# Attention in units of 64 queries of four heads, with queries and keys in plain float32, in place of units of 128 queries of two heads in split float32r

## The chip, the cores and the metric

The kernel runs on one core of a Trainium2 chip. The metric is the time of one execution on the device, in microseconds. Three runs of the kernel before took 944.76, 943.54 and 944.8 us, median 944.76. TensorE is called PE here, VectorE DVE, ScalarE ACT, GpSimd POOL, and SP is the engine that issues the transfers.

## The reference

```python
# attention: q, k, v of (4 batches, 8 heads, 576 positions, 64 features)
scores = 0.125 * q @ k.T                    # per batch and head
scores = where((rel >= 0) & (rel < 128), scores - slope[h] * abs(rel), -1e9)   # rel = query - key
x = softmax(scores) @ v                     # 2304 tokens x 512 features
# first MoE layer, dense
h = x @ w_in                                # 512 -> 2048
x = maximum(0.01 * h, h) @ w_out            # 2048 -> 512
# second MoE layer: 8 experts, each token goes to one, 288 tokens an expert (greedy by logit)
logits = x @ w_gate
out[tokens of e] = maximum(x @ w1[e], 0) @ w2[e]
```

A query sees itself and the 127 positions before it, in its own batch of 576 positions. w_in and w_out are handed to the kernel as 64-bit floating-point numbers and become float32 on the chip, in pieces ("conversions", `conv_abs` to `in_low`). Routing is exact enough only with products near float32, so the MoE products are made of float32r parts: a value is a high part (a rounded copy, made by ACT) and a low part (the difference, made by DVE or POOL), and three products, high by high, low by high, high by low, stand for one.

## The kernel before

The 2304 tokens are 18 blocks of 128 queries (`NB`), counted through the four batches, so that a batch's end falls within blocks 4 and 13, at row 64. A *unit* is one block with one pair of heads: 72 units, four to a block. A step s of the loop at L664 takes unit s through the softmax and, at the same time, makes the scores of unit s + 1, the transposes of unit s - 1 and the products with v of unit s - 2. Beside them a step holds at most one *item*, 24 matmuls of the first MoE product (`expand`, L532), and at set step numbers the stages of a conversion (`conv_at`, steps 0 to 45, two steps in three), the gate's products made from w_out (`gate_transpose`, `gate_product`, `gate_fold`), and the logits (L559) and their folds (L570). An item of chunk c (two blocks) can start when the chunk's last products with v are done (`ready`). When the units end, items alone go on until L223, the second product, takes over at 444 us.

PE's and ACT's instructions run in the order in which the program writes them (`manual_schedule`); those of DVE, POOL and SP are put in order by a planner that estimates when each can run, and that lets a load wait for a free buffer while others pass.

The parts that the change touches:

- `load_half` (L315) loads queries and keys of half a block's heads, 64 features high, twice, into partitions 0 to 63 and 64 to 127. `split_half` (L403 to L417) copies the keys to the high part on ACT (L413) and subtracts for the low part (L414), both on all 128 partitions. Of the queries ACT makes the high part (L415) and L416 turns partitions 64 to 127 into the low part. The subtractions run on DVE for the first three halves (`SPLIT_V`) and on POOL after that.
- `scores` (L429): a head's query tile (high part over low part, 128 rows) meets the high keys and then the low keys, two float32r matmuls of 256 columns that add up, so four for a unit (L443). Where a block crosses a batch's end (`CUT`) a third matmul of one row adds a bias from `marks`. Blocks with fewer than 128 older keys of their batch take L448, a pair of matmuls for each part.
- `softmax_exp` and `softmax_norm`: for each head L464 scales, adds the bias and takes the minimum on DVE, L467 is the exponential on ACT with its sum, L475 and L476 make the reciprocal on DVE, and L478 multiplies.
- `transpose_p` (L488) makes four transposes of 128x128 for a unit; ACT copies them out (L491).
- `weighted` (L507): for each head and each of its two sets of 128 keys a plain float32 matmul of 128 queries into the partitions 0 to 63 or 64 to 127 of `xv`. A plain float32 matmul leaves two matmul records in the trace. In block 14, and 5, one set has 64 keys and stands between sets of 128.
- `bias_sb`: eight biases of 384 columns, two made on DVE and six on POOL (L632).
- POOL has, beside the splits, the sum of each conversion (L367) and the low part of w_in (L372).

Of the kernel before, what the change touches and what calls it, by code (L numbers as in the profile page):

```python
# [35 lines left out]
SPLIT_V = range(3)  # L36
# [40 lines left out]

OLD = [min(i * P % S, P) for i in range(NB)]  # L80
CUT = [S - i * P % S if S - i * P % S < P else None for i in range(NB)]


def _consts():
# [16 lines left out]
    rel = r[:, None] + P - np.arange(2 * P)[None, :]  # L101
    rel = np.where((rel >= 0) & (rel < WINDOW), -8.0 * rel, -2e12)
    add("rel", np.concatenate([rel, rel[:, :P]], axis=1))
# [15 lines left out]

_r, _cut = np.arange(P), next(c for c in CUT if c)  # L120
assert all(c in (None, _cut) for c in CUT)
MARKS = np.concatenate([_r >= _cut, np.full(P, -2e30), np.where(_r < _cut, -2e30, 0), np.full(P, -2e30)])
MARKS = MARKS[None].astype(mybir.dt.np(BF16))


@with_exitstack
def tile_attn_moe_moe2(ctx: ExitStack, tc: tile.TileContext, qk, v, w_in, w_out, w_gate, w1, w2, consts, mark_rows, out):
# [175 lines left out]
    with ExitStack() as actx:  # L303
        apool = actx.enter_context(tc.tile_pool(name="apool", bufs=2))
        marks = apool.tile([1, 4 * P], BF16, name="marks", bufs=1)
# [7 lines left out]
        half, vtile, qtile, raws = {}, {}, {}, {}  # L313

        def load_half(i, hf):  # L315
            if i < NB:
                t = apool.tile([P, 2, 4, P], F32, tag="qk", name=f"qk_{i}_{hf}", bufs=3)
                src = qk[i, :, :, 4 * hf:4 * hf + 4, :]
                nc.sync.dma_start(t[:D], src)
                nc.sync.dma_start(t[D:], src)  # L320
                half[i, hf] = t

        def load_v(i):
            if i < NB:
                for j, n in ((0, P),) + (((1, P - CUT[i]),) if CUT[i] else ()):
                    t = apool.tile([P, DM], F32, tag="v", name=f"v_{i}_{j}", bufs=4)
                    nc.sync.dma_start(t[:n], v[(i + 1) * P - n:(i + 1) * P, :])
                    vtile[i, n] = t
# [74 lines left out]
        def split_half(i, hf):  # L403

            if i >= NB:
                return
            if hf == 0:
                qtile[i] = apool.tile([P, H, P], F32R, tag="qs", name=f"qs_{i}")
            t, qs = half.pop((i, hf)), qtile[i]
            hs = slice(4 * hf, 4 * hf + 4)  # L410
            kh, kl = (r[:, hs, i % 2, :] for r in kring)
            eng = V if 2 * i + hf in SPLIT_V else GP
            A.activation(kh, t[:, 1], AF.Copy)  # L413
            eng.tensor_tensor(out=kl, in0=t[:, 1], in1=kh.bitcast(F32), op=ALU.subtract)  # L414
            A.activation(qs[:, hs, :], t[:, 0], AF.Copy)  # L415
            eng.tensor_tensor(out=qs[D:, hs, :], in0=t[D:, 0], in1=qs[D:, hs, :].bitcast(F32),  # L416
                              op=ALU.subtract)  # L417

        def keys_of(i):

            keys = [(i % 2, 0, vtile[i, P], P)]
            if OLD[i]:
                old = ((i - 1) % 2, P - OLD[i], vtile[i - 1, OLD[i]], OLD[i])
                keys = keys + [old] if OLD[i] == P and i % 2 == 0 else [old] + keys
            return keys

        st = {}

        def scores(u):  # L429
            i, c = u  # L430
            keys = keys_of(i)
            s = bank("s", "s_%d_%d" % u).rearrange("p (h k) -> p h k", h=2)
            whole = OLD[i] == P
            for h in range(2):
                hd = 2 * c + h
                q = qtile[i][:, hd, :]
                if whole:
                    ends = [(q, r[:, hd].rearrange("p a k -> p (a k)")) for r in kring]
                    if CUT[i]:
                        bo = P * (i % 2 == 0)  # L440
                        ends.append((marks[:, :P], marks[:, P + bo:3 * P + bo]))
                    for x, (a, b) in enumerate(ends):
                        T.matmul(s[:, h, :], a, b, start=(x == 0), stop=(x == len(ends) - 1))  # L443
                    continue
                ko = 0
                for slot, kc, _, kn in keys:
                    for x, ring in enumerate(kring):
                        T.matmul(s[:, h, ko:ko + kn], q, ring[:, hd, slot, kc:kc + kn],  # L448
                                 start=(x == 0), stop=(x == 1))
                    ko += kn  # L450
            st[u] = dict(keys=keys, whole=whole, s=s)

        def softmax_exp(u):
            i, c = u
            d = st[u]
            nk = P + OLD[i]
            bo = P if d["whole"] and i % 2 == 0 else P - OLD[i]
            nm_ = "%d_%d" % u
            neg = apool.tile([P, 2, 256], F32, tag="neg", name=f"neg_{nm_}")
            nm = apool.tile([P, 2], F32, tag="nm", name=f"nm_{nm_}", bufs=4)  # L460
            sm = apool.tile([P, 2], F32, tag="sm", name=f"sm_{nm_}", bufs=4)
            pr = apool.tile([P, 2, 256], F32, tag="pr", name=f"pr_{nm_}", bufs=PRB)
            for h in range(2):
                V.tensor_tensor_reduce(  # L464
                    out=neg[:, h, :nk], in0=d["s"][:, h, :nk], in1=bias_sb[:, 2 * c + h, bo:bo + nk],
                    scale=-0.125, scalar=3e38, op0=ALU.add, op1=ALU.min, accum_out=nm[:, h:h + 1])
                A.activation(pr[:, h, :nk], neg[:, h, :nk], AF.Exp, scale=-1.0, bias=nm[:, h:h + 1],  # L467
                             accum_out=sm[:, h:h + 1])
            d.update(nk=nk, sm=sm, pr=pr)

        def softmax_norm(u):
# [5 lines left out]
            for h in range(2):  # L477
                V.tensor_scalar(pr[:, h, :nk], pr[:, h, :nk], rs[:, h:h + 1], None, op0=ALU.mult)  # L478

        def transpose_p(u):  # L480
            d = st[u]
            keys, pr = d["keys"], d["pr"]
            pt = bank("t", "pt_%d_%d" % u).rearrange("p (h b q) -> p h b q", h=2, b=2)
            pts = apool.tile([P, 2, 2, P], F32, tag="pts", name="pts_%d_%d" % u, bufs=PTB)
            ko = 0
            for kb, (_, _, _, kn) in enumerate(keys):
                for h in range(2):
                    T.transpose(pt[:kn, h, kb, :], pr[:, h, ko:ko + kn], ident)  # L488
                ko += kn
            if d["whole"]:  # L490
                A.activation(pts, pt, AF.Copy)  # L491
            else:
                for kb, (_, _, _, kn) in enumerate(keys):
                    A.activation(pts[:kn, :, kb, :], pt[:kn, :, kb, :], AF.Copy)
# [4 lines left out]
        def weighted(u):  # L499
# [3 lines left out]
            if c == 0:  # L503
                xv[i] = bank("v", f"xv_{i}", bufs=1).rearrange("p (c q) -> p c q", c=4)
# [639 lines left out]
```

## Time and profile before

| | |
|---|---|
| profiled execution | 944.32 us, of which the span of instructions 942.5 |
| median of three runs | 944.76 us (943.54 to 944.8) |
| PE busy | 885.2 us, 94% |
| DVE busy | 634.0 us, 67% |
| ACT busy | 414.8 us, 44% |
| POOL busy | 211.9 us, 22% |
| mean granted clock of PE | 0.986 |

A busy time is the time in which an instruction of that engine is in progress. Matmuls overlap and their ends are modelled, so a PE that is busy all the time need not be at its peak: the distance from one start to the next tells how fast it goes. A DVE instruction that is held up counts as busy while it is held; the same instruction's shorter cases show what it needs. In a row of a group "xcount | busy, mean ns of one | idle before" follow the names and shapes.

### The profile page before, as it was taken

How to read it: one execution, taken by the hardware profiler on the slowest of the kernel's cores; microseconds unless marked ns; L12 is line 12 of the kernel's file. 1: busy time of each engine (PE TensorE's matmuls, PEld its weight loads, DVE VectorE, ACT ScalarE, POOL GpSimd, SP SyncE). 2: the span in 40 equal slices, each digit the busy share in tenths (PEclk: the TensorE clock that was granted, in tenths of full speed). 3: DMA queues.
4: the chain of work that ended last, by engine and by line, in shares of the span. 5: the costliest groups of instructions: out<-in, count | busy, mean ns of one | idle time of the engine just before them, and what ended most of it. 6: DMA issues, size and time to landing. Idle time of an engine off the chain costs nothing.

```text
span 942.5 us, 17809 instructions
## 1 busy us (share of the span) xinstructions
PE 885.2 (94%) x6886; PEld 759.8 (81%) x6886; DVE 634.0 (67%) x1569; ACT 414.8 (44%) x865; POOL 211.9 (22%) x198
## 2 busy tenths in 40 slices
PE   2677999999999999999999999998999999999996
PEld 2455888999898888898777766775789999999995
DVE  6999999999965455435877877777316455555550
ACT  5555665667654445434212121211215555565551
POOL 4565554454422222000000000000011211122211
PEclk9998899999999999999999999999999999999998
DMA  9555486787549965246332434221325556666540
GB/s 253 157 139 151 114 224 191 215 237 213 176 118 262 244 170 141 81 134 192 122 136 78 136 100 135 90 80 67 101 92 176 190 169 191 223 207 192 181 134 26
DMA packets 100727, 146.98 MB, mean 156 GB/s; under 512 B 6561, under 2 KB 64162, under 8 KB 100642
## 3 DMA queue, kind: packets, MB, share of 16 engines
q1 hardware_dynamic: 97570, 136.40, 49.6%
q0 software_dynamic: 3072, 9.44, 2.9%
q8 instruction: 54, 0.88, 0.4%
q14 instruction: 31, 0.25, 0.1%
HBM read 113.04 MB, written 32.77 MB: 155 GB/s over the span
## 4 chain that ended last, share of the span: by engine, by line
PE 80%; DVE 14%; issue 4%; POOL 1%; DMA 1%; ACT 0%; SPq 0%; POOLq 0%; DVEq 0%; ACTq 0%
PE po L223 21%; PE h L532 19%; PE m L1024 10%; PE y L1043 10%; PE xv L507 4%; PE s L443 3%; PE cnt L844 3%; PE pt L488 3%; PE lg L559 2%; DVE dt L357 2%; DVE pr L478 2%; DVE rs L475 2%; DVE neg L464 1%; DVE dt L355 1%; DVE de L365 1%
## 5 line engine op out<-in xcount | busy, mean ns | idle before, releaser
L223 PE MATMUL po<-wh_out,gol 128*128 128x512 f32 x272 | 112.6, 414 | 4.6 <-DVE gol L191 4.6
L223 PE MATMUL po<-wh_out,goh 128*128 128x512 f32 x272 | 111.0, 408 | 0.0
L223 PE MATMUL po<-wl_out,goh 128*128 128x512 f32 x272 | 110.6, 407 | 0.0
L532 PE MATMUL h<-xh,wh_in 128*128 128x256 f32 x576 | 100.1, 296 | 0.0
L532 PE MATMUL h<-xl,wh_in 128*128 128x256 f32 x576 | 92.9, 284 | 3.2 <-DVE xl L518 3.2
L532 PE MATMUL h<-xh,wl_in 128*128 128x256 f32 x576 | 92.6, 283 | 0.0
L183 ACT ACTIVATE goh<-gin 128x1024 fp32r<-128x1024 f32 x34 | 36.0, 1060 | 124.8 <-DMA gin<-g_dram 112.0
L160 DVE TENSOR_TENSOR wl_w<-st_w,wh_w 128x1024 fp32r<-128x1024 f32 x60 | 72.9, 1224 | 25.9 <-ACT wh_w L159 25.9
L545 DVE TENSOR_TENSOR gb<-h,th 128x512 f32<-128x512 f32 x72 | 49.4, 686 | 57.8 <-ACT th L541 56.9
L532 PEld LDWEIGHTS h<-xl,wh_in 128*128 128x128 f32 x576 | 79.3, 190 | 3.4 <-DVE xl L518 3.4
L532 PEld LDWEIGHTS h<-xh,wh_in 128*128 128x128 f32 x576 | 78.6, 191 | 3.7 <-issue 2.5
L478 DVE TENSOR_SCALAR pr<-pr,rs 128x256 f32<-128x256 f32 (+2 forms) x144 | 80.0, 599 | 1.3
L532 PEld LDWEIGHTS h<-xh,wl_in 128*128 128x128 f32 x576 | 79.4, 190 | 0.0
L1043 PE MATMUL y<-hh,wh_w 128*128 128x288 f32 x256 | 77.4, 302 | 0.0
L1043 PE MATMUL y<-hh,wl_w 128*128 128x288 f32 x256 | 75.6, 295 | 0.0
L1043 PE MATMUL y<-hl,wh_w 128*128 128x288 f32 x256 | 75.5, 295 | 0.0
L488 PE MATMUL pt<-cst,pr 128*128 128x128 f32 (+1 forms) x272 | 47.8, 296 | 28.8 <-DVE pr L478 28.4
L256 POOL DMA_INDIRECT xg<-x_dram,idx x3 | 3.0, 990 | 309.7 <-DMA x_dram<-xo 309.0
L467 ACT ACTIVATE pr<-neg,nm 128x256 f32<-128x256 f32 (+2 forms) x144 | 68.9, 483 | 0.3 <-DVE nm L464 0.3
L541 ACT ACTIVATE th<-h 128x512 f32<-128x512 f32 x72 | 42.9, 596 | 57.1 <-PE h L532 57.0
L414 POOL TENSOR_TENSOR k_l<-qk,k_h 128x512 fp32r<-128x512 f32 x33 | 44.6, 1352 | 103.3 <-ACT k_h L413 103.2
L1063 POOL DMA_INDIRECT out_dram<-ys,idx x24 | 27.6, 1150 | 170.4 <-ACT ys L1058 168.5
(234 smaller groups left out, 2030.2 us busy)
## 6 DMA issues: line engine op xcount, KB each, us to landing
st_w<-in_w_dram SPq DMA_DIRECT2D x64, 512.0 KB, 4.1
qk<-in_qk_dram SPq DMA_DIRECT2D x72, 256.0 KB, 4.8
g_dram<-gb SPq DMA_DIRECT2D x72, 256.0 KB, 3.5
gin<-g_dram SPq DMA_DIRECT2D x34, 512.0 KB, 3.8
gr<-g_dram SPq DMA_DIRECT2D x20, 512.0 KB, 8.2
raw<-in_w_in_dram SPq DMA_DIRECT2D x16, 512.0 KB, 4.7
raw<-in_w_out_dram SPq DMA_DIRECT2D x16, 512.0 KB, 4.8
v<-in_v_dram SPq DMA_DIRECT2D x18, 256.0 KB, 4.4
```

The lines of the kernel that those rows point to most:

```text
L160: lo_engine.tensor_tensor(out=wl, in0=st, in1=wh.bitcast(F32), op=ALU.subtract)
L223: T.matmul(po, g, w, start=(k == 0), stop=(k == 47))
L414: eng.tensor_tensor(out=kl, in0=t[:, 1], in1=kh.bitcast(F32), op=ALU.subtract)
L467: A.activation(pr[:, h, :nk], neg[:, h, :nk], AF.Exp, scale=-1.0, bias=nm[:, h:h + 1], accum_out=sm[:, h:h + 1])
L478: V.tensor_scalar(pr[:, h, :nk], pr[:, h, :nk], rs[:, h:h + 1], None, op0=ALU.mult)
L488: T.transpose(pt[:kn, h, kb, :], pr[:, h, ko:ko + kn], ident)
L507: T.matmul(xv[i][h * D:(h + 1) * D, c, :], vk[:kn, (2 * c + h) * D:(2 * c + h + 1) * D], pts[:kn, h, kb, :], start=(kb == 0), stop=(kb == ...
L532: T.matmul(hp[:, j, :], w[:, d, j * P:(j + 1) * P], x[:, d, :], start=(k == 0), stop=(k == 11))
L541: A.activation(th, hp, AF.Copy, scale=0.01)
L545: V.tensor_tensor(out=gbs[c][:, o:o + 2, :], in0=hp, in1=th, op=ALU.max)
L1024: T.matmul(hp, w[:, d, :], x[:, d, :], start=(k == 0), stop=(k == 11))
L1043: T.matmul(yp, w, x[:, f, :], start=(k == 0), stop=(k == 23))
```

## The change

A unit becomes one block of 64 queries (`Q`, 36 blocks, nine to a batch) with two pairs of heads: two units to a block, 72 in all, and the loop's step numbers stay. A block sees at most 192 keys, and only keys of its own batch: 64 for a batch's first block, 128 for its second. Keys and queries come laid out with two heads on the 128 partitions. The query tile of a head pair has two versions, each with the other head's 64 rows set to zero once by POOL, so that a matmul over 128 rows gives one head's scores; the two heads of a pair write partitions 0 to 63 and 64 to 127 of the scores. These are plain float32 matmuls of 64 weight columns and up to 192 moving columns, four for a unit. Nothing is split; `split_half`, `marks` and their loads go. The softmax, on 128 partitions (64 queries of two heads) twice for a unit, has up to 192 columns. The keys of a block are cut into one set of 64 or 128 or two of 96 for the transposes (four for most units) and the products with v: eight plain float32 matmuls of 64 moving columns for most units, the two heads alternating. Keys of a batch stay in one tile, loaded 192 at a time with as many queries, every third block; v is loaded for each block with all its keys. The biases are four of 192 columns, two on DVE and two on POOL.

```diff
-SPLIT_V = range(3)
+Q = 64
+NQ = N // Q
+SQ = S // Q
+LD = 3 * Q
+def keys_before(j):
+    return Q * min(j % SQ + 1, 3)
...
-        bias_sb = apool.tile([P, H, 3 * P], BF16, name="bias_sb", bufs=1)
-        kring = [apool.tile([P, H, 2, P], F32R, name=f"k_{x}", bufs=1) for x in "hl"]
+        bias_sb = apool.tile([P, H // 2, 3 * Q], BF16, name="bias_sb", bufs=1)
+        qring = [apool.tile([P, 2, H // 2, LD], F32, name=f"q_{x}", bufs=1) for x in range(2)]
...
+        def load_qk(n, ps=((0, 4),)):
+            if n >= N // LD:
+                return
+            b, m = divmod(n, S // LD)
+            if m == 0 and b not in ktile:
+                ktile[b] = apool.tile([P, H // 2, S], F32, tag="k", name=f"k_{b}")
+            for c0, c1 in ps:
+                nc.sync.dma_start(ktile[b][:, c0:c1, m * LD:(m + 1) * LD], k_in[n, :, c0:c1, :])
+                for a in range(2):
+                    rows = slice(a * D, a * D + D)
+                    nc.sync.dma_start(qring[n % 2][rows, a, c0:c1, :], q_in[n, rows, c0:c1, :])
+        def load_v(j):
+            if j < NQ:
+                nk = keys_before(j)
+                kn = nk if nk <= P else nk // 2
+                t = apool.tile([P, 2, DM], F32, tag="v", name=f"v_{j}", bufs=3)
+                vtile[j] = [(x, kn, t[:kn, x, :]) for x in range(nk // kn)]
+                end = (j + 1) * Q
+                nc.sync.dma_start(t[:kn, :nk // kn, :], v[end - nk:end, :].rearrange("(x p) d -> p x d", p=kn))
...
-            for h in range(2):
-                hd = 2 * c + h
-                q = qtile[i][:, hd, :]
-                if whole:
-                    ends = [(q, r[:, hd].rearrange("p a k -> p (a k)")) for r in kring]
...
+            s = bank("s", "s_%d_%d" % u)[:, :2 * nk].rearrange("p (x k) -> p x k", x=2)
+            qt, t0 = qring[j // 3 % 2], j % 3 * Q
+            for x in range(2):
+                c = 2 * hf + x
+                for a in range(2):
+                    T.matmul(s[a * Q:a * Q + Q, x, :], qt[:, a, c, t0:t0 + Q],
+                             ktile[b][:, c, (m + 1) * Q - nk:(m + 1) * Q], start=True, stop=True)
...
-            for kb, (_, _, _, kn) in enumerate(keys):
-                for h in range(2):
-                    T.transpose(pt[:kn, h, kb, :], pr[:, h, ko:ko + kn], ident)
+            for x in range(2):
+                for kb, kn, _ in keys:
+                    T.transpose(pt[:kn, x, kb, :], pr[:, x, kb * kn:kb * kn + kn], ident)
+            A.activation(pts[:kn, :, :len(keys), :], pt[:kn, :, :len(keys), :], AF.Copy)
...
-            for h in range(2):
-                for kb, (_, _, vk, kn) in enumerate(keys):
-                    T.matmul(xv[i][h * D:(h + 1) * D, c, :],
-                             vk[:kn, (2 * c + h) * D:(2 * c + h + 1) * D], pts[:kn, h, kb, :],
+            for x in range(2):
+                c = 2 * hf + x
+                for kb, _, vk in keys:
+                    for a in range(2):
+                        T.matmul(xv[i][a * D:a * D + D, c, q0:q0 + Q], vk[:, (2 * c + a) * D:(2 * c + a + 1) * D],
+                                 pts[:vk.shape[0], x, kb, a * Q:a * Q + Q],
...
+            for t in qring:
+                GP.memset(t[D:, 0], 0.0)
+                GP.memset(t[:D, 1], 0.0)
-            load_half(0, 0)
+            load_qk(0, ((0, 2),))
             nc.sync.dma_start(cst[:, :late_consts], consts[:, :late_consts])
-            load_half(0, 1)
             load_v(0)
+            load_qk(0, ((2, 4),))
             load_raw(0)
             load_raw(1)
-            load_half(1, 0)
+            load_v(1)
             load_raw(2)
-            load_v(1)
+            load_qk(1)
...
             def prepare(u):
-                i, c = u
-                if c == 2:
-                    split_half(i + 1, 0)
-                    load_half(i + 1, 1) if i else None
...
+                j, hf = u
+                if hf == 0:
+                    load_v(j + 2)
+                    if j and j % 3 == 0:
+                        load_qk(j // 3 + 1)
```

## Rows read from the trace of the kernel before

**Rows 1.** Busy time by stretch: start:end, length, each engine, PE clock, DMA share, GB/s
```profile
13.80:153.20 139.40, 107.17 (x725) 87.15 (x726) 136.35 (x321) 82.03 (x213) 77.95 (x59) 0.95 0.60 164
153.20:257.30 104.10, 103.91 (x969) 94.44 (x968) 101.30 (x279) 69.59 (x173) 45.55 (x34) 1.00 0.75 215
257.30:394.10 136.80, 136.80 (x1272) 116.89 (x1274) 77.87 (x247) 68.92 (x183) 28.92 (x23) 1.00 0.66 174
```

**Rows 2.** The chain of waits from 13.8 to 153.2 us, by line
```profile
by line: DVE pr L478 12.6%; DVE dt L357 12.0%; PE h L532 9.4%; DVE rs L475 9.3%; DVE neg L464 8.3%; issue 7.8%; DVE dt L355 6.5%; DVE de L365 5.7%; DVE gb L545 3.9%; PE s L443 3.9%; DVE de L364 3.4%; DVE dt L356 3.3%; PE xv L507 3.0%; PE pt
```

**Rows 3.** Groups of DVE from 13.8 to 153.2 us: busy us, mean ns
```profile
L478 DVE TENSOR_SCALAR pr<-pr,rs 128x256 f32<-128x256 f32 (+2 forms) x52 | 32.6, 672 | 0.2
L357 DVE SCALAR_TENSOR_TENSOR dt<-raw,dt 128x512 int32<-128x512 int32 x18 | 20.0, 1112 | 0.0
...
L475 DVE TENSOR_SCALAR rs<-sm 128x2 f32<-128x2 f32 x26 | 16.5, 635 | 0.1
```

**Rows 4.** One line each, whole span: duration in ns, min/median/max
```profile
L478 DVE TENSOR_SCALAR pr<-pr,rs x144: 273/348/1453, 15.3 to 394.8; 128x256 f32<-128x256 f32 x112, 128x128 f32<-128x128 f32 x16, 128x192 f32<-128x192 f32 x16
...
L475 DVE TENSOR_SCALAR rs<-sm x72: 150/166/1272, 13.8 to 394.2; 128x2 f32<-128x2 f32 x72
...
L357 DVE SCALAR_TENSOR_TENSOR dt<-raw,dt x32: 677/693/1774, 14.1 to 251.1; 128x512 int32<-128x512 int32 x32
```

**Rows 5.** Groups of POOL from 13.8 to 153.2 us
```profile
L367 POOL TENSOR_TENSOR dt<-dt,de 128x512 f32<-128x512 f32 x18 | 23.5, 1304 | 53.1 <-DVE de L365 34.3 <-DVE rs L475 10.3 <-ACT pr L467 3.4
L372 POOL TENSOR_TENSOR wl_in<-dt,wh_in 128x512 fp32r<-128x512 f32 x14 | 19.2, 1374 | 0.9
L414 POOL TENSOR_TENSOR k_l<-qk,k_h 128x512 fp32r<-128x512 f32 x12 | 16.6, 1379 | 3.3 <-ACT k_h L413 3.3
L416 POOL TENSOR_TENSOR qs<-qk,qs 64x512 fp32r<-64x512 f32 x12 | 16.3, 1362 | 0.9
```

**Rows 6.** Groups of DVE from 13.8 to 153.2 us, shapes kept apart
```profile
L464 DVE CUSTOM_DVE_ANT_0 neg<-s,bias_sb 128x256 f32<-128x256 f32 x40 | 15.3, 412 | 0.7 <-PE s L443 0.6
...
L464 DVE CUSTOM_DVE_ANT_0 neg<-s,bias_sb 128x192 f32<-128x192 f32 x8 | 2.5, 347 | 0.0
```

**Rows 7.** DVE in order of time at the start: start us, us
```profile
11.27 0.69 DVE L416 TENSOR_TENSOR qs<-qk,qs 64x512 fp32r<-64x512 f32 x1
11.99 0.29 DVE L464 CUSTOM_DVE_ANT_0 neg<-s,bias_sb 128x128 f32<-128x128 f32 x1
```

**Rows 8.** PE in order of time, products with v and scores of one step
```profile
361.03 0.67 PE L507 MATMUL xv<-pts,v 128*64 128x128 f32 x8
361.63 0.39 PE L443 MATMUL s<-k_h,qs 128*128 128x256 f32 x1
361.85 0.28 PE L443 MATMUL s<-k_l,qs 128*128 128x256 f32 x1
361.97 0.28 PE L443 MATMUL s<-k_h,qs 128*128 128x256 f32 x1
...
362.20 0.28 PE L532 MATMUL h<-xh,wh_in 128*128 128x256 f32 x1
```

**Rows 9.** PE, records of v begun by 185.45 us, and by 185.60
```profile
185.41 0.34 PE L507 MATMUL xv<-pts,v 128*64 128x128 f32 x2
...
185.41 0.45 PE L507 MATMUL xv<-pts,v 128*64 128x128 f32 x4
```

**Rows 10.** PE in order of time, four logits and the scores behind them
```profile
300.84 1.93 PE L559 MATMUL lg<-gr,wg 128*32 128x256 f32 x32
302.71 0.30 PE L448 MATMUL s<-k_h,qs 128*128 128x64 f32 x1
```

**Rows 11.** PE in order of time, scores with marks (six matmuls, the first shown)
```profile
290.11 0.39 PE L443 MATMUL s<-k_h,qs 128*128 128x256 f32 x1
...
291.40 0.39 PE L532 MATMUL h<-xh,wh_in 128*128 128x256 f32 x1
```

**Rows 12.** PE in order of time, products with v of 64 and 128 rows in turn
```profile
323.55 1.51 PE L507 MATMUL xv<-pts,v 64*64 64x128 f32 x8
```

More of the change, by code (lines that the diff above doesn't have):

```diff
@@ L117, with tile_attn_moe_moe2 @@
 COLS, CONSTS = _consts()
[L120 to L123, printed above, removed]
 @with_exitstack
-def tile_attn_moe_moe2(ctx: ExitStack, tc: tile.TileContext, qk, v, w_in, w_out, w_gate, w1, w2, consts, mark_rows, out):
+def tile_attn_moe_moe2(ctx: ExitStack, tc: tile.TileContext, q_in, k_in, v, w_in, w_out, w_gate, w1, w2, consts, out):
     nc = tc.nc
@@ L453, in softmax_exp @@
+            st[u] = dict(nk=nk, s=s)
         def softmax_exp(u):
[L454 removed]
+            j, hf = u
             d = st[u]
[L456 to L457 removed]
+            nk = d["nk"]
             nm_ = "%d_%d" % u
[L459 removed]
+            neg = apool.tile([P, 2, 3 * Q], F32, tag="neg", name=f"neg_{nm_}")
             nm = apool.tile([P, 2], F32, tag="nm", name=f"nm_{nm_}", bufs=4)
@@ L499, in weighted @@
         def weighted(u):
-            i, c = u
-            d = st.pop(u)
-            keys, pts = d["keys"], d["pts"]
-            if c == 0:
+            j, hf = u
+            i, q0 = j // 2, j % 2 * Q
+            pts, keys = st.pop(u)["pts"], vtile[j]
+            if j % 2 == 0 and hf == 0:
                 xv[i] = bank("v", f"xv_{i}", bufs=1).rearrange("p (c q) -> p c q", c=4)
-            for h in range(2):
-                for kb, (_, _, vk, kn) in enumerate(keys):
-                    T.matmul(xv[i][h * D:(h + 1) * D, c, :],
-                             vk[:kn, (2 * c + h) * D:(2 * c + h + 1) * D], pts[:kn, h, kb, :],
-                             start=(kb == 0), stop=(kb == len(keys) - 1))
-            if c == 3:
+            for x in range(2):
+                c = 2 * hf + x
[3 more added lines that the diff above has]
+                                 pts[:vk.shape[0], x, kb, a * Q:a * Q + Q],
+                                 start=(kb == 0), stop=(kb == len(keys) - 1))
+            if j % 2 == 1 and hf == 1:
                 if i % 2 == 0:
@@ L587, in late_logits @@
                 logits(c, f4, t[:, f4 % 2 * 4:f4 % 2 * 4 + 4, :], "t")
-        units = [(i, c) for i in range(NB) for c in range(4)]
+        units = [(j, hf) for j in range(NQ) for hf in range(2)]
         items = [(c, fp) for c in range(NCH) for fp in range(8)]
@@ L1120, in _layout @@
         "consts": CONSTS,
-        "marks": MARKS,
     }
```

120 lines of the change are left out of this document (27 added, 93 removed).

## The prediction

> **What bounds the kernel now.** I read the page first, then the busy times by stretch, then the chain of waits of the first one, then single groups. Attention and the first products of the first MoE run to 444 us; what follows does not change, so the question is what those 444 us become. They have two parts with different limits. From the first softmax at 13.8 us to 153.2 us (units 0 to 25, stretch A) DVE is busy 136.4 of 139.4 us and PE 107.2. From there to 257.3 us (units 26 to 45, B) and to 394.1 us (units 46 to 71, C) PE is busy without a gap, and DVE has room [rows 1]. The chain of A says the same: L478 and L357, both DVE's, lead it, and of its first five lines only the third is PE's [rows 2].
>
> DVE in A is not full of work, it is full of waiting. L475 adds a constant to 128x2 numbers and takes 635 ns there in the mean, 166 ns in the median of the whole kernel; L478 672 against 348, L357 1112 against 693 [rows 3, 4]. The excess is 26 x 0.469 + 52 x 0.324 + 18 x 0.419 = 12.2 + 16.8 + 7.5 = 36.5 us. At such times POOL is in a TENSOR_TENSOR: A has 56 of them, 1.30 to 1.38 us each, and 24 are the low parts of keys and queries (L414, L416) [rows 5]. So one POOL instruction costs DVE 36.5 / 56 = 0.65 us.
>
> **The change, part by part.** *The splits go.* L413 to L416 vanish: 24 POOL instructions of A, worth 24 x 0.65 = 15.6 us of DVE. Bounds: nothing, if DVE then waits for the other 32, and all of the 1.37 us that one lasts, 33 us. I take 15.6, which lies at the three measured groups. ScalarE loses two copies for each half block; it is 82 us busy of A, so that buys nothing.
>
> *Less softmax.* A unit was 128 queries of two heads with up to 256 keys and is now 64 queries of four heads with up to 192; there are 72 units both ways, so every step that is keyed to the unit's number stays. L464 falls from 412 to 347 ns, as the 192-wide ones of today show [rows 6]: 36 x 0.065 = 2.3 us in A, and about 1 us more for the units at a batch's start with 64 or 128 keys. With L478's narrower form uncounted, A is 15.6 + 3.4 = 19 us shorter, 120 us. DVE would then need 136.4 - 19 = 117, and PE 107.2 + 26 x 0.17 (below) = 112: neither stops it sooner.
>
> *The start.* The first L464 runs at 12.0 us, behind a split instruction of DVE that ended at 11.96 [rows 7]. Without it L464 waits for the constants and the first keys, whose transfers are 0.4 MB in place of 0.5; six POOL biases become two. The first conversion still waits for its raw weights. I take 3 us, between 0 and 5.
>
> *PE, one unit.* Today the products with v and the scores take from 361.03 to 362.20, 1.17 us: 0.60 for eight records of v (each plain float32 product leaves two), 0.57 for four float32r scores [rows 8]. Records of the two column halves run in pairs, each further pair 0.11 us later (0.34 us for one pair, 0.45 for two), at 128 columns [rows 9]. New scores: four products of 192 columns, eight records, four pairs of 0.11 x 192/128 = 0.165, so 0.66. The logits bound this from above: 32 records in four column groups, 256 wide, from 300.84 to 302.71, are 0.234 for a group, 0.175 at 192 columns, 0.70 in all [rows 10]. New products with v: sixteen records of 64 columns, eight pairs of 0.055 = 0.44 as today, if a weight load of 64 columns also fits beside 0.055; the trace shows it beside 0.11 alone, so the other end is a pair that stays at 0.11, 0.44 more a unit. I take the first: of the two, loads and moving columns, it is the moving ones to which today's spacing answers (0.11 at 128, 0.234 at 256). The transposes keep their 128 moving columns: nothing. Changing between column shapes costs: the eight records of v leave 0.16 of their 0.60 to the two changes, and the first score takes 0.22 to the next where others take 0.12 [rows 8], so 0.10 before and 0.10 behind it. With v and scores now in one shape the change moves behind the scores: same number. Per unit 0.05 + 0.44 + 0.66 + 0.19 = 1.34, 0.17 more than today.
>
> *PE, changes of shape that are added.* Where something in full width or in column quarters lies between v and the scores (the gate's products in B, logits and their folds in C), the scores today follow it with at most one change; now they need one before (0.14) and one behind (0.20). By the code's order I count +0.28 a step in B, 20 steps, 5.6 us, and about 4 us in C.
>
> The Trainium skill, "TensorEngine Tiling (Array Packing)", section Key Properties, says that changing the tiling mode drains the engine: a rule against this change. The trace agrees with 0.10 us on each side of a change [rows 8], and without that rule B and C would come out 10 us lower.
>
> *PE, what disappears.* The blocks that cross a batch are dear. Four units of C pay two extra products with marks: 290.11 to 291.40, 1.29 in place of 0.57, 0.72 x 4 = 2.9 us [rows 11]. Four units multiply 64 rows and 128 rows of keys in turn: 1.51 in place of 0.67, 0.84 x 4 = 3.4 us [rows 8, 12]. Four new units of C with 64 or 128 keys save some 3 us.
>
> B: 16 x 0.17 + 5.6 - 1 (its four short units) = +7. C: 22 x 0.17 + 4 - 2.9 - 3.4 - 3 = -2. Together +5; bounds -5 (no added change of shape) and +22 (a weight load that is not hidden, 38 x 0.44 = 17).
>
> *Transfers.* Keys and queries come once in place of twice (9.4 MB for 18.9), v almost three times (12.6 for 5.0): 2 MB less. DMA is at 0.60 to 0.75 of its share in A to C [rows 1]; each v is asked for four steps ahead, some 20 us. I cost this at nothing; if the wait for a free v buffer (three, released by the products two units back) leaves a load late, the products with v wait, a few us in all.
>
> **Sum**, from the profiled execution's 944.3 us (span 942.5, 1.8 around it; the median of the runs is 944.76): -3 - 19 + 5 = -17, so 927 us.
>
> **Rivals.**
> 1. *DVE was blocked for the whole of POOL's instruction*, and each one removed gives back more. For it: single L475 of up to 1.27 us [rows 4]. Against: the mean of 0.65. A then falls until PE stops it, at 112 us: -27 in place of -19, 919 us. The Trainium skill, "SBUF — State Buffer", section Who interferes with whom, calls the shared port an exclusive lock held for the whole instruction; the long L475 agree, the mean shows that DVE often finds other work first.
> 2. *The room in A is not used.* ScalarE's and PE's answers between softmax and transposes set the step, or DVE meets POOL's other 32 instructions more often. For it: L478 feeds PE's transposes and leads the chain of A [rows 2]. Against: DVE's idle time in A is 3 us in all. A gains a third, 6: 940 us.
> 3. *A 64-column weight load does not hide behind 64 moving columns.* +17 in B and C, A unharmed: 944 us, no change.
> 4. *The slower side: the two column halves run one after the other for the scores* (both write one bank, each with its own queries, against the same keys). Then the change does not do what it says: eight records in a row, 0.66 more a unit. It decides from the point where PE has no gap, all of B and C: 38 x 0.66 = +25; PE's need in A grows to 107.2 + 26 x 0.83 = 129, so A gives only 10. 944.3 - 3 - 10 + 5 + 25 = 961 us. Against: v's records pair in one bank today [rows 9].
>
> **Numbers.** Forecast 0.50 (by itself 917 to 937: both ends of the start, half of the shape changes, a few us in A), rival 1 0.13, rival 2 0.15, rival 3 0.08, rival 4 0.12, the rest 0.02. A difference under 0.2%, 1.9 us, cannot be told from none. Faster: 0.50 + 0.13 + 0.15 and 0.02 of rival 3 = 0.80; same 0.05 (rival 3); slower 0.15. Range 913 to 948: it takes in rivals 1 to 3 and leaves out rival 4 and the tails.
>
> **What would show it.** After: unit 26 begins near 131 us in place of 153; L475's mean in A falls towards 0.4 us; no L414 or L416 on POOL; scores in four pairs about 0.165 apart, v in pairs 0.055 apart; 0.2 between the last score and the first product h; B about 111 us, C about 135. Wrong if records of the halves do not pair, if A's DVE is idle while the step does not shorten, or if PE waits for a load of keys or v.

## The result, and the profile after

The changed kernel takes 920.07 us in the median of four runs (919.47 to 920.97), beside 944.78 us for the kernel before on the same chip (four runs, 943.54 to 945.26). The ratio is 0.974, with a 95% interval of 0.972 to 0.976: 24.7 us faster. The forecast was 927 us with a range of 913 to 948.

The profiled execution took 919.52 us, with a span of 917.7. PE is busy 874.0 us of it (885.2 before), DVE 561.7 (634.0), ACT 367.5 (414.8), POOL 119.0 (211.9). Cut at the starts of the first `rs` instruction on DVE (L475 before, L443 after) of units 0, 26, 46 and 71, the two executions stand like this, in us:

| | before | after | difference | forecast |
|---|---|---|---|---|
| start | 13.8 | 12.1 | -1.7 | -3 |
| A, units 0 to 25 | 139.4 | 112.9 | -26.5 | -19 |
| B, units 26 to 45 | 104.1 | 109.1 | +5.0 | +7 |
| C, units 46 to 70 | 136.8 | 136.1 | -0.8 | -2 |
| last unit, items and all that follows | 548.4 | 547.6 | -0.8 | 0 |

The busy times by stretch, after, with the columns of [rows 1]; the fourth row runs from the last unit to the first L221 (L223 before), the second product of the first MoE layer:

```profile
12.10:125.00 112.90, 92.41 (x939) 75.72 (x940) 108.57 (x319) 65.11 (x183) 42.40 (x33) 0.97 0.69 201
125.00:234.10 109.10, 109.10 (x1171) 94.33 (x1170) 80.50 (x281) 57.00 (x152) 18.10 (x14) 1.00 0.68 195
234.10:370.10 136.00, 136.00 (x1520) 116.00 (x1522) 57.90 (x245) 54.08 (x158) 0.53 (x1) 1.00 0.64 173
370.10:420.50 50.40, 50.40 (x480) 45.64 (x471) 22.68 (x32) 17.98 (x26) 0.00 (x0) 1.00 0.51 156
```

B and C are PE's without a gap, as before. In A DVE is still the busiest, 108.6 of 112.9 us, and is 27.8 us less busy than before; PE is busy 92.4 us of A, 14.8 less. The chain of waits of A, by line, answers to [rows 2]: PE's L498 now leads with 19.3%, and each of DVE's lines has fallen behind it. The load of q in the chain is one of 3.77 us from 103.01 us on; PE works through it without a gap.

```profile
by line: PE h L498 19.3%; DVE dt L361 7.9%; DVE pr L446 7.2%; DVE rs L443 6.8%; PE s L418 6.8%; DVE neg L432 6.7%; PE pt L456 6.4%; PE xv L473 5.9%; DVE dt L359 5.9%; issue 5.4%; DVE de L369 4.8%; DMA q<-in_q_dram 3.3%; DVE de L368 3.2%; DV
```

The groups of DVE in A (12.1 to 125 us) that answer to [rows 3, 6] follow. All four mean times have fallen. Those of L446 and L443 still stand well above the medians of the whole kernel, which come after them; L361 has 784 ns for a median of 692, and L432, at 327 for 349, shows no excess.

```profile
L446 DVE TENSOR_SCALAR pr<-pr,rs 128x192 f32<-128x192 f32 (+2 forms) x52 | 19.4, 414 | 0.2
L432 DVE CUSTOM_DVE_ANT_0 neg<-s,bias_sb 128x192 f32<-128x192 f32 (+2 forms) x52 | 15.5, 327 | 2.6 <-PE s L418 2.5
L361 DVE SCALAR_TENSOR_TENSOR dt<-raw,dt 128x512 int32<-128x512 int32 x18 | 14.1, 784 | 0.0
L443 DVE TENSOR_SCALAR rs<-sm 128x2 f32<-128x2 f32 x26 | 12.9, 495 | 0.2
```

One line each over the whole span (minimum, median and maximum in ns), answering to [rows 4]:

```profile
L446 DVE TENSOR_SCALAR pr<-pr,rs x144: 245/314/1431, 13.7 to 370.8; 128x192 f32<-128x192 f32 x112, 128x64 f32<-128x64 f32 x16, 128x128 f32<-128x128 f32 x16
...
L443 DVE TENSOR_SCALAR rs<-sm x72: 154/166/1278, 12.1 to 370.1; 128x2 f32<-128x2 f32 x72
```

POOL in A, answering to [rows 5], has 32 instructions in place of 56:

```profile
L371 POOL TENSOR_TENSOR dt<-dt,de 128x512 f32<-128x512 f32 x18 | 23.4, 1298 | 69.1 <-DVE de L369 30.9 <-ACT pr L435 15.0 <-ACT wh_in L353 10.0
L376 POOL TENSOR_TENSOR wl_in<-dt,wh_in 128x512 fp32r<-128x512 f32 x14 | 18.7, 1339 | 1.1
```

PE in order of time in C, one step, answering to [rows 8]: the products with v go from 345.47 on, and the two views of it that end at 345.59 and 345.65 hold four and six records, two more for each 0.06 us. So the records come in pairs that stand 0.058 us apart. A record does not name its column half; that the two of a pair belong to different halves is read from the spacing.

```profile
345.47 0.34 PE L473 MATMUL xv<-pts,v 96*64 96x64 f32 x4
...
345.47 0.39 PE L473 MATMUL xv<-pts,v 96*64 96x64 f32 x6
```

The scores of the unit before do the same. Six records have begun by 341.57 and eight by 341.73, and the first product h starts at 341.98. The third pair begins at 341.56, the fourth at 341.72: 0.163 apart, forecast 0.165. From the first score to h it is 0.80 us, of which 0.26 lie between the last pair and h, forecast 0.2.

```profile
341.18 0.71 PE L418 MATMUL s<-k,q 128*64 128x192 f32 x6
...
341.18 0.87 PE L418 MATMUL s<-k,q 128*64 128x192 f32 x8
341.98 0.75 PE L498 MATMUL h<-xh,wh_in 128*128 128x256 f32 x4
```

In a step of C with nothing between v and the scores, the two take 1.27 us, for 1.34 in the forecast and 1.17 in the kernel before:

```profile
311.73 0.69 PE L473 MATMUL xv<-pts,v 96*64 96x64 f32 x16
312.25 0.82 PE L418 MATMUL s<-k,q 128*64 128x192 f32 x8
313.00 0.39 PE L498 MATMUL h<-xh,wh_in 128*128 128x256 f32 x1
```

### The profile page after: what moved, and what is told of

It reads as the page before. It is cut to its first block, busy times and chain, and to the rows that moved or that the text cites. A ratio compares the mean times of both kernels' runs of the same rounds, so it can differ in the third digit from the quotient of the medians.

```text
span 917.7 us, 18945 instructions
## 1 busy us (share of the span) xinstructions
PE 874.0 (95%) x7590; PEld 746.6 (81%) x7590; DVE 561.7 (61%) x1563; ACT 367.5 (40%) x785; POOL 119.0 (13%) x132
## 4 chain that ended last, share of the span: by engine, by line
PE 85%; DVE 9%; issue 3%; DMA 1%; POOL 1%; SPq 0%; ACT 0%; POOLq 0%; DVEq 0%; ACTq 0%
PE po L221 22%; PE h L498 22%; PE m L983 10%; PE y L1002 10%; PE s L418 4%; PE xv L473 4%; PE pt L456 3%; PE cnt L803 3%; PE lg L525 2%; DVE dt L361 1%; PE wtp L386 1%; DVE pr L446 1%; PE yo L1012 1%; DVE rs L443 1%; DVE neg L432 1%
## 5 line engine op out<-in xcount | busy, mean ns | idle before, releaser
L221 PE MATMUL po<-wh_out,gol 128*128 128x512 f32 x272 | 112.1, 412 | 4.6 <-DVE gol L189 4.6
L221 PE MATMUL po<-wh_out,goh 128*128 128x512 f32 x272 | 110.7, 407 | 0.0
L221 PE MATMUL po<-wl_out,goh 128*128 128x512 f32 x272 | 110.3, 406 | 0.0
L498 PE MATMUL h<-xh,wh_in 128*128 128x256 f32 x576 | 103.7, 302 | 0.5 <-ACT xh L483 0.5
L511 DVE TENSOR_TENSOR gb<-h,th 128x512 f32<-128x512 f32 x72 | 49.5, 687 | 85.6 <-ACT th L507 84.2
L498 PE MATMUL h<-xl,wh_in 128*128 128x256 f32 x576 | 91.8, 281 | 0.0
L498 PE MATMUL h<-xh,wl_in 128*128 128x256 f32 x576 | 91.6, 281 | 0.0
L498 PEld LDWEIGHTS h<-xh,wh_in 128*128 128x128 f32 x576 | 77.2, 189 | 17.4 <-issue 11.9
L457 ACT ACTIVATE pts<-pt 96x512 f32<-96x512 f32 (+2 forms) x72 | 39.2, 545 | 101.8 <-PE pt L456 101.7
L498 PEld LDWEIGHTS h<-xl,wh_in 128*128 128x128 f32 x576 | 78.5, 188 | 0.2 <-DVE xl L484 0.2
L498 PEld LDWEIGHTS h<-xh,wl_in 128*128 128x128 f32 x576 | 78.4, 188 | 0.0
L418 PE MATMUL s<-k,q 128*64 128x192 f32 (+2 forms) x576 | 62.5, 340 | 6.6 <-DMA q<-in_q_dram 6.6
L456 PE MATMUL pt<-cst,pr 128*96 128x128 f32 (+2 forms) x256 | 43.2, 289 | 22.4 <-DVE pr L446 22.4
L221 PEld LDWEIGHTS po<-wh_out,gol 128*128 128x128 f32 x272 | 51.4, 189 | 15.9 <-DVE gol L189 6.3
L157 ACT ACTIVATE wh_w<-st_w 128x1024 fp32r<-128x1024 f32 x60 | 62.5, 1053 | 1.7 <-DMA st_w<-in_w_dram 1.7
L371 POOL TENSOR_TENSOR dt<-dt,de 128x512 f32<-128x512 f32 x32 | 41.5, 1296 | 161.7 <-DVE de L369 90.2
```

The source lines that it names most:

```text
L157: A.activation(wh, st, AF.Copy)
L221: T.matmul(po, g, w, start=(k == 0), stop=(k == 47))
L371: (V if k in ADD_V else GP).tensor_tensor(out=t, in0=t, in1=e, op=ALU.add)
L418: T.matmul(s[a * Q:a * Q + Q, x, :], qt[:, a, c, t0:t0 + Q], ktile[b][:, c, (m + 1) * Q - nk:(m + 1) * Q], start=True, stop=True)
L456: T.transpose(pt[:kn, x, kb, :], pr[:, x, kb * kn:kb * kn + kn], ident)
L457: A.activation(pts[:kn, :, :len(keys), :], pt[:kn, :, :len(keys), :], AF.Copy)
```

## The experiments

Each is an edit of the changed kernel, or of the kernel before where it says so. Lengths of A, B and C are cut as in the table above. The kernel before ran beside each of them: its median was 943.32 us beside the first four, 942.9 beside the next four and 943.9 beside the last two, against 944.78 in the result. So times of different groups, and those set beside the 920.07, can differ by 1 to 2 us without any edit; the lengths of stretches come from one execution of each.

**POOL's splits put back as idle work.** In each second unit POOL again subtracts twice, on a tile that nobody reads.

```diff
...
+                e = A.activation(pr[:, x, :nk], neg[:, x, :nk], AF.Exp, scale=-1.0, bias=nm[:, x:x + 1],
+                                 accum_out=sm[:, x:x + 1])
+            if hf == 1 and j > 2:
+                for r in (slice(0, P), slice(D, P)):
+                    g = GP.tensor_tensor(out=junk[r, 2], in0=junk[r, 0], in1=junk[r, 1], op=ALU.subtract)
+                    tc.add_manual_dep(g.ins, e.ins.name, SYNC, reason="as the split waited for its copy")
...
```

> The changed kernel with the POOL work of the splits put back as idle work: in every second unit from the fourth block on, two subtractions of 128x512 and 64x512 on POOL over a scratch tile, each behind that unit's exponential; nobody reads their result. Theory (the gain of the first stretch is DVE freed from POOL): that stretch, 112.9 us in the changed kernel, goes back by 24 x 0.65 to 24 x 0.8 = 16 to 19 us, L443's mean from 495 ns towards 635, and the stretches behind it, where PE has no gap, hardly move: 936 to 940 us. Rival (the gain is the narrower softmax and the removed copies and marks): POOL's work is off the path, within 2 us of the changed kernel's 920.

936.29 us (936.1 to 937.18), 16.2 above the changed kernel. A has 20 of the instructions, for 24 of the splits before, and is 128.9 us long, 16.0 more; B is 1.5 longer and C 1.0 shorter. Groups of DVE in A:

```profile
L451 DVE TENSOR_SCALAR pr<-pr,rs 128x192 f32<-128x192 f32 (+2 forms) x52 | 26.2, 543 | 0.2
L362 DVE SCALAR_TENSOR_TENSOR dt<-raw,dt 128x512 int32<-128x512 int32 x18 | 17.7, 982 | 0.0
L448 DVE TENSOR_SCALAR rs<-sm 128x2 f32<-128x2 f32 x27 | 15.5, 575 | 0.5 <-ACT pr L436 0.4
```

The instructions put back, in the groups of POOL in A:

```profile
L440 POOL TENSOR_TENSOR junk<-junk 128x512 f32<-128x512 f32 (+1 forms) x20 | 27.4, 1370 | 12.8 <-ACT pr L436 12.0
```

DVE's own work is unchanged, and the same three groups are longer again: its busy time in A rises from 108.57 to 122.44, 0.69 us for each POOL instruction, and the stretch by 0.80 for each. POOL's work alone carries most of the change's gain: 16.0 of the 26.5 us of A with 20 of the 24 instructions.

**The scores right behind the products with v**, ahead of the gate's products and the logits, so that v and scores share one column shape.

```diff
+                scores(units[1])
...
                     elif s + 1 < len(units):
-                        scores(units[s + 1])
                         prepare(units[s + 1])
...
+                if s + 2 < len(units):
+                    scores(units[s + 2])
```

> The changed kernel with each unit's scores made right behind the products with v of the step before, ahead of the gate's products and logits, so that both column-half groups of PE stand side by side and the change of shape between them goes. Theory (a change of shape costs 0.1 us on each side, and the changed kernel adds some two of them in steps with gate products or logits): 0.28 us in some 25 steps and about 4 us behind them, 7 to 10 us less: 910 to 913 us, all of it after unit 26. Rival (the added changes hide behind waits that PE has anyway): within 2 us of 920.

912.07 us (910.77 to 913.09), ratio to before 0.967 (0.965 to 0.969). A is 113.7 us, 0.7 longer; B is 104.9 and C 131.7, 4.2 and 4.35 less than in the changed kernel. One step of B on PE in order of time, in the changed kernel:

```profile
131.26 0.69 PE L473 MATMUL xv<-pts,v 96*64 96x64 f32 x16
131.87 0.43 PE L395 MATMUL pg<-wt,gsb 128*32 128x128 f32 x8
132.23 0.66 PE L386 MATMUL wtp<-cst,dt 128*128 128x128 f32 x4
132.82 0.87 PE L418 MATMUL s<-k,q 128*64 128x192 f32 x8
133.62 0.75 PE L498 MATMUL h<-xh,wh_in 128*128 128x256 f32 x4
```

The same work with the scores moved:

```profile
131.74 0.69 PE L473 MATMUL xv<-pts,v 96*64 96x64 f32 x16
132.26 0.82 PE L418 MATMUL s<-k,q 128*64 128x192 f32 x8
133.01 0.43 PE L395 MATMUL pg<-wt,gsb 128*32 128x128 f32 x8
133.37 0.66 PE L386 MATMUL wtp<-cst,dt 128*128 128x128 f32 x4
133.78 0.72 PE L498 MATMUL h<-xh,wh_in 128*128 128x256 f32 x4
```

From the first v to h the same matmuls take 2.36 us in the one order and 2.04 in the other. Start to start, v falls from 0.61 to 0.52, the scores from 0.80 to 0.75, the transposes of weights (L386) from 0.59 to 0.41. The products with v and the transposes lose the change of shape that stood behind them; the scores still have one behind them, to the gate's products, and give the least. So the added changes were there, 8.5 us in all against 9.6 in the forecast.

**POOL quiet.** The sums and the low parts of the conversions go from POOL to DVE.

```diff
-ADD_V = ()
-IN_V = (0, 1)
+ADD_V = range(32)
+IN_V = range(16)
```

> The changed kernel with POOL's last work beside attention, the 32 sums and 14 low parts of the conversions, moved to DVE, where such an instruction takes about 0.68 us when POOL is quiet. Theory (one POOL instruction costs DVE 0.65 to 0.8 us): in the first stretch DVE loses 32 x 0.72 = 23 us of being held and gains 32 x 0.68 = 22 us of work, so within 3 us of 920; the 495 ns mean of L443 falls to about 160. If one POOL instruction holds DVE for its whole 1.3 us: 32 x (1.3 - 0.68) = 20 us less, about 900 us, or as far as PE allows, 905. Rival (DVE's waits are not POOL's): L443 stays near 495 ns and the stretch grows by 22 us, 940 us.

918.79 us (918.72 to 918.95), ratio to before 0.974 (0.972 to 0.976), the same as the changed kernel's; A is 111.6 us, 1.4 less, and B 0.5 longer. The row of A by stretch:

```profile
11.90:123.50 111.60, 91.23 (x935) 75.14 (x936) 103.10 (x352) 64.15 (x183) 0.42 (x1) 0.94 0.72 206
```

Groups of DVE in it, two of them POOL's before:

```profile
L371 DVE TENSOR_TENSOR dt<-dt,de 128x512 f32<-128x512 f32 x18 | 12.3, 686 | 0.0
...
L376 DVE TENSOR_TENSOR wl_in<-dt,wh_in 128x512 fp32r<-128x512 f32 x16 | 11.0, 688 | 0.0
...
L443 DVE TENSOR_SCALAR rs<-sm 128x2 f32<-128x2 f32 x27 | 4.4, 164 | 0.3
```

L443 is at its median in A too, 164 ns in place of 495, so its excess was POOL's. DVE has taken on 22.0 us of work (32 instructions by 0.69) and is yet 5.5 us less busy, so each POOL instruction had cost it 0.86 us. But A hardly gains: with 8.5 us of DVE's time free, other waits set the step. The longest is before L511 (gb), 3.2 us for ACT's th, which ACT makes from PE's h, where it was 0.2; what shortening it would give, no run shows.

**The kernel before without its low parts.** L414 and L416 are left out, the low keys are set to zero once, and the copies by ACT stay.

```diff
             A.activation(kh, t[:, 1], AF.Copy)
-            eng.tensor_tensor(out=kl, in0=t[:, 1], in1=kh.bitcast(F32), op=ALU.subtract)
             A.activation(qs[:, hs, :], t[:, 0], AF.Copy)
-            eng.tensor_tensor(out=qs[D:, hs, :], in0=t[D:, 0], in1=qs[D:, hs, :].bitcast(F32),
-                              op=ALU.subtract)
...
+            GP.memset(kring[1].bitcast(F32), 0.0)
```

> The kernel before without the subtractions that make the low parts of queries and keys (L414 and L416): the low keys are zero and the lower half of the query tile stays a second high part, so the scores come out twice as large; all loads, copies, matmuls and transfers stay. Theory (POOL's splits were what the first stretch paid for): 24 x 0.65 to 24 x 0.8 off the first stretch, with three split pairs less on DVE another 2, and nothing off the stretches behind it: 923 to 928 us. Rival (the narrower softmax and the new form of the scores bring the gain): 940 us or more.

926.98 us (925.19 to 931.04), ratio 0.983 (0.980 to 0.986). A is 123.9 us, 15.5 less than before; B 2.5 less, C 1.7 more. A in its three parts (units 0 to 9, 10 to 17, 18 to 25), by stretch:

```profile
13.70:56.00 42.30, 26.09 (x121) 18.65 (x122) 39.27 (x120) 27.78 (x75) 15.36 (x14) 0.89 0.75 202
56.00:95.40 39.40, 35.55 (x264) 30.03 (x263) 37.26 (x98) 26.18 (x65) 14.29 (x11) 0.90 0.60 172
95.40:137.60 42.20, 42.20 (x345) 37.68 (x344) 39.17 (x105) 27.99 (x73) 13.17 (x10) 1.00 0.71 194
```

The same three parts in the changed kernel:

```profile
12.10:53.00 40.90, 27.48 (x222) 18.52 (x223) 37.99 (x120) 22.58 (x66) 14.64 (x13) 0.92 0.77 211
53.00:86.90 33.90, 27.47 (x334) 23.73 (x333) 33.27 (x98) 20.39 (x56) 14.54 (x11) 1.00 0.65 203
86.90:125.00 38.10, 37.45 (x387) 33.47 (x386) 37.31 (x104) 22.14 (x61) 13.21 (x10) 1.00 0.65 189
```

DVE is relieved of 20.7 us (136.35 to 115.69), 0.80 for each of the 24 POOL instructions when the two subtractions that were DVE's own (0.77 and 0.69 us) are taken off. The stretch gives back only 15.5 of it; the other 5.2 are idle time of DVE. Of these 2.3 are in units 18 to 25, where PE is now busy 42.2 of 42.2 us: there the old form's matmuls are the bound. The changed kernel has 38.1 us there, with PE at 37.45. Another 2.7 are in units 0 to 9, where PE is not full: DVE waits there 1.5 us for scores, at a granted clock of 0.50 (the lower of its two levels, from 46.5 us on, just behind 2.10 us in which PE stood idle), and 1.0 us for the copy that begins a conversion.

**ACT's copies put back as idle work**, two in each second unit.

```diff
...
+            if hf == 1 and j > 2:
+                for r in range(2):
+                    A.activation(junk[:, 1 + r], junk[:, 0], AF.Copy)
...
```

> The changed kernel with the splits' two copies of 128x512 put back on ACT as idle work, in every second unit from the fourth block on, behind that unit's exponentials; nobody reads them. Theory (ACT is off the path, as the forecast costed it): 24 copies of 0.62 us in the first stretch fit beside 113 us of which ACT is busy 65, so within 2 us of 920. Rival (ACT answers in its written order, and the copies stood between the exponentials and the copies of the transposes, so part of the 7.5 us that the first stretch gained over the forecast is theirs): 924 to 928 us, with the first stretch 4 to 8 us longer.

919.52 us (918.96 to 919.72), and A is 112.9 us with 20 of the copies, as without them. The copies that went were worth nothing.

**The second and third edit together**, scores behind v and POOL quiet.

> The changed kernel with the scores right behind the products with v and with the conversions' POOL work on DVE, both edits at once. Theory: they act in different stretches, the first by 8 us where PE has no gap, the second by 1 us in the first stretch, and add up: 910 to 912 us. Rival (with DVE's own work grown and the scores made earlier the first stretch meets a new wait): 913 us or more.

910.88 us (909.21 to 911.93), ratio 0.966 (0.964 to 0.968), with A 111.0, B 105.4 and C 131.6. This is the best version, 8 to 9 us below the changed kernel (8 by the ratios to before); from the one with the scores moved alone it cannot be told.

**The halves in turn**: the scores written one column half after the other.

```diff
-            for x in range(2):
-                c = 2 * hf + x
-                for a in range(2):
+            for a in range(2):
+                for x in range(2):
+                    c = 2 * hf + x
```

> The changed kernel with the four scores of a unit in another order: both of one column half, then both of the other. Theory (PE runs the two halves side by side whatever their order in the program, as it did for the products with v in the kernel before, whose order was one half, then the other): within 2 us of 920. Rival (matmuls begin in the program's order, so only neighbours pair): the eight records of a unit run nearly one after the other, 0.3 to 0.66 us more a unit where PE has no gap, 38 units, 11 to 25 us, and some in the first stretch: 931 to 950 us.

920.35 us (919.24 to 921.31), no difference. One step of C, PE in order of time, in stretches that end at 342.37, 342.57 and 342.58, and the product h behind them:

```profile
342.35 0.39 PE L418 MATMUL s<-k,q 128*64 128x192 f32 x2
...
342.35 0.54 PE L418 MATMUL s<-k,q 128*64 128x192 f32 x3
...
342.35 0.55 PE L418 MATMUL s<-k,q 128*64 128x192 f32 x4
...
343.16 0.75 PE L498 MATMUL h<-xh,wh_in 128*128 128x256 f32 x4
```

The records still come in pairs, the second of a pair 0.013 us behind the first where the alternating order has 0.006, and first score to h is 0.81 us, for 0.80 with the alternating order. So this edit did not make the halves run in turn, and it prices no serial order; it shows that the order in the program does not decide the time that the eight records take.

**The kernel before with a narrower softmax**: on top of the one without low parts, at most 192 of the 256 score columns go through the softmax.

```diff
-            nk = P + OLD[i]
+            nk = min(P + OLD[i], 192)
...
```

> The kernel before without the low parts, as in the earlier run of 927 us, and with the softmax of its 256-wide units over 192 columns alone (the last 64 columns are left out, and the second transpose reads columns of the first again, so that all matmuls stay). Theory: DVE gains 0.065 us in L464 and some 0.04 in L478, four instructions a unit, 36 + 36 of them in the first stretch, 4 to 5 us: 922 us, first stretch 119 us in place of 124; the rest, to the changed kernel's 113, is PE's (blocks across a batch's end) and ACT's. Rival (all of the rest is the narrower softmax): first stretch 113 us, 916 us.

922.38 us (921.31 to 926.14). A is 121.1 us, 2.8 less than without this edit, where 119 was expected; B and C stay. Nothing of the 2.8 is in units 18 to 25, which stay at 42.3 us with PE full.

**The same without marks**: the matmuls of one row at a batch's end are left out.

```diff
-                    if CUT[i]:
-                        bo = P * (i % 2 == 0)
-                        ends.append((marks[:, :P], marks[:, P + bo:3 * P + bo]))
```

> The kernel of the earlier run of 922 us (the kernel before, no low parts, softmax over 192 columns) without the matmuls with marks in blocks 4 and 13 (the bias that separates two batches is left out). Theory (what the first stretch gained beyond POOL and the narrower softmax is PE's dear blocks at a batch's end, which lie in it too): each of eight units loses 0.72 us, 2.9 us in the first stretch (121.1 to 118.2) and 2.9 behind unit 46 (138.6 to 135.7): 916.5 us. Rival (DVE alone sets the first stretch): its length stays, only the later 2.9 us come: 919.5 us.

919.66 us (918.92 to 919.82): C 3.3 less, A 1.7 less. The forecast had 2.9 for C. Of A the expectation had 2.9 too, and its rival nothing; what came lies between, 1.3 of it in units 10 to 17.

**The same with the key sets grouped**: both heads' products with the first set, then both with the second, so that 64 and 128 rows no longer take turns within a head.

```diff
-            for h in range(2):
-                for kb, (_, _, vk, kn) in enumerate(keys):
+            for kb, (_, _, vk, kn) in enumerate(keys):
+                for h in range(2):
```

> The same without marks, and with the products with v in another order: both heads' first set of keys, then both heads' second. In blocks 5 and 14, whose sets are of 64 and 128 rows, the shape then changes once in a unit in place of three times, and the halves can pair. Theory: such a unit falls from 1.51 us towards 0.9, four units in the first stretch and four behind unit 46: 2 to 3 us in each, 911 to 913 us, first stretch about 115.5. Rival (DVE sets the first stretch there): 2 to 3 us in all, 914 us.

913.08 us (911.5 to 914.41): 6.6 below the one without this edit. In the profiled executions C is 3.0 shorter, A 0.9 (118.6 us, where 115.5 was expected), the start 0.6 and B 0.4; the rest of the difference lies between single runs. Units 18 to 25, where the grouped sets of A lie, are 1.8 shorter; units 10 to 17, in which this edit changes nothing, are 1.2 longer. A unit with sets of 64 and 128 rows, PE in order of time, without this edit:

```profile
299.24 1.51 PE L501 MATMUL xv<-pts,v 64*64 64x128 f32 x8
```

And with it:

```profile
297.32 0.81 PE L501 MATMUL xv<-pts,v 64*64 64x128 f32 x8
```

0.70 us a unit, with the same eight records: the cost was the taking of turns. The kernel before, without splits and with these cheap edits, comes to within 3 us of the best version; it leaves out the low parts, the marks and a part of the keys, so it does less than either kernel.

## Why the prediction was right, and where its sum was not

The time came out 7 us below the forecast and inside the range that the forecast had by itself (917 to 937). The mechanism held: A is DVE's stretch, DVE was held by POOL, and PE pays a little in B. Of the signs named in advance (forecast in brackets), unit 26 begins at 125.0 us (131), L443's mean in A is 495 ns (towards 400), B is 109.1 us (111) and C 136.1 (135). The terms of the sum:

- *The start*, -1.7 for -3. L432 no longer waits for a split and runs at 5.87 us in place of 11.99. But the first exponential stands behind the first conversion's copy (L346) in ACT's order, and that one waits for its raw weights until 10.61 us. That the conversion waits stood in the forecast; the value taken was too large.
- *A*, -26.5 for -19: this is the mis-sized term. The experiments part it like this: the low parts 15.5, the narrower softmax 2.8, the marks 1.7, the grouped sets 0.9, and 5.6 that is left between the last of these (118.6 us) and the changed kernel (112.9). The first two are near their forecast (15.6 and 3.4), but that the 15.6 fits is luck: two errors of opposite sign. The price of a POOL instruction was too low, 0.65 us, because only three of the held groups were summed. Two more, L355 and L356, have medians of 418 and 426 ns and means of 658 and 624 in the same stretch; with 4.3 and 3.6 us of theirs the excess is 44.4 us, 0.79 for each of the 56. The runs gave 0.69, 0.80 and 0.86. (That POOL is the cause shows in the trace before as well: of the 26 L475 of A the 13 that took over 0.3 us all overlap an instruction of POOL, of the others two.) And the step "DVE would then need 117 and PE 112: neither stops it sooner" failed: with DVE relieved, PE is the bound of the old form in units 18 to 25, and some waits for PE open in units 0 to 9.
- What the forecast had not counted is that the change relieves PE just there: it had PE's need in A rise from 107 to 112 us, and PE is busy 92.4. The blocks at a batch's end lie in A as well (units 16 to 23), and the savings on them were summed for C alone. By thirds, 118.6 against 112.9 is 0.3 us in units 0 to 9, 3.2 in 10 to 17 and 2.2 in 18 to 25. In the last third PE is busy 40.17 of 40.3 us in the version with grouped sets and 37.45 of 38.1 in the changed one; by the forecast's own prices that is four short units (about -3) and four long ones at +0.17, -2.3. Of the 3.2 us in units 10 to 17, 2.45 are one wait of DVE for PE's scores, which stand behind an item and the products with v while the granted clock is 0.50, the lower of its two levels (84.4 to 87.8 us; PE had stood idle for 2.62 us up to 83.98). In the version whose sets are not grouped the same wait is 0.94, with the clock at 1.00, and the third takes 35.9 us for 37.1. In the changed kernel the scores of that unit are short, and DVE does not wait. The last third and the wait with grouped sets, then the wait without them:

```profile
91.00:131.30 40.30, 40.17 (x346) 36.40 (x345) 37.68 (x106) 27.74 (x73) 13.16 (x10) 1.00 0.66 186
...
88.89 0.36 DVE L458 CUSTOM_DVE_ANT_0 neg<-s,bias_sb 128x192 f32<-128x192 f32 x1 [2.45 <-PE s L437]
...
88.53 0.36 DVE L458 CUSTOM_DVE_ANT_0 neg<-s,bias_sb 128x192 f32<-128x192 f32 x1 [0.94 <-PE s L437]
```

So about 1.2 us of the 5.6 seem to go with where the low clock falls; no run holds the clock still. It differs between the two kernels as well: 0.84 in units 10 to 17 before, 1.00 after. Before, it fell to 0.50 there twice, at 80.7 us, in 4.25 us of idle time of PE, and at 94.4, just behind 2.65 us of it. DVE was busy 41.66 of 43.6 us there, so waits for a slow PE can have been at most 1.9 us of A's gain.
- *ACT* costs nothing, as forecast and shown by the copies put back.
- *B and C*, +5.0 and -0.8 for +7 and -2. The spacing of pairs was right (0.163 and 0.058 for 0.165 and 0.055). The added changes of shape were 4.2 and 4.35 us for 5.6 and 4. Without them B is 0.8 above before, for +1.4 (a long unit costs 0.10 more in the step shown, for 0.17), and C 5.1 below, for -6; marks and sets were 3.3 and 3.0 for 2.9 and 3.4. The Trainium skill, "TensorEngine Tiling (Array Packing)", section Key Properties, with its drain at a change of tiling mode, spoke against this change, and the trace agrees with 0.32 us in the step shown.
- *Transfers*, nothing, as forecast: 145.1 MB for 147.0 in the whole kernel, and from 12.1 to 420 us PE waits for no load. Its waits there, by the view of waits:

```profile
PE pt L456 <- DVE pr L446: 22.4, 10, 4.3
PE h L498 <- ACT xh L483: 0.5, 1, 0.5
```

The rivals. The first (DVE blocked for the whole of POOL's instruction) gave 919 us, nearer than the forecast, and A, at 112.9 us, came to its 112; but that is luck. Its price is refuted, 0.69 to 0.86 us of 1.37, and what it let stop A, PE at 112, is not there: PE is busy 92.4 us of A, and with POOL quiet 103.1 us of DVE's work took 111.6 us. The Trainium skill, "SBUF — State Buffer", section Who interferes with whom, with its lock for the whole instruction, agrees with the longest L443 (1278 ns); it gives no price in the mean, and that is what the runs measured. The second (the room is not used) is refuted for the splits, of which 15.5 of 20.7 us came back; for the last 32 POOL instructions it holds, as the quiet POOL showed. The third is refuted by the 0.058, the fourth by the 0.163 between pairs. A serial order of the halves was not had, so its price was not measured.

## What to carry to other kernels

Where a shared resource holds an engine, sum the excess over all the groups that it holds, in the stretch where it binds, and then recount the next engine's need in each part of that stretch: a mean over it (PE 107 of 139 us) hid that PE was full in the last third once DVE was relieved. Savings on rare steps are counted in every stretch in which such steps occur. Work in column halves or quarters is put side by side in the engine's order: the same matmuls took 8.5 us less when nothing of another shape stood between them.

## What the runs showed of the hardware that was not expected

- The scores of two column halves took the same 0.8 us whether the program alternated the halves or wrote one after the other; only the second record of a pair began 0.013 us behind the first in place of 0.006.
- Plain float32 products of 64 rows and of 128 rows that take turns cost 1.51 us for eight records, and 0.81 us when they are grouped by rows.
- Moving 32 instructions of 1.3 us from POOL to DVE, where they take 0.69 us each, made DVE 5.5 us less busy: what POOL held it up for was more than the work itself.
